# Second early expert with its rows as stationary operand, and full tails in the first Fourier transform

## The chip, the cores and the metric

The kernel runs on one core of one Trainium2 chip. The metric is device time in microseconds (us) of one execution, as a median of several. The engines are named as in the profile: PE (TensorE, with PEld for its weight loads), DVE (VectorE), ACT (ScalarE), POOL (GpSimd) and SP (SyncE, which here only asks for DMA transfers).

## The reference

Attention over 576 positions in 4 batches and 8 heads of 64, each query looking at the last 128 keys; a mixing layer with a Fourier transform over positions and features, a normalisation and an MLP; and a layer of 8 experts in which each token goes to one.

```python
scores = where(mask, scale * q @ k.T + bias, -1e9)          # rel in [0, 128)
x = (softmax(scores) @ v)                                    # (4, 576, 512)

X = np.fft.fft(np.fft.fft(x, axis=1), axis=2)
u = x + np.real(X)
un = (u - mean(u)) / sqrt(var(u) + 1e-6)
x = u + np.maximum(un @ w_ch1, 0.0) @ w_ch2                  # 512 -> 2048 -> 512

e = argmax(logits[b, s]) if s == 0 or local_gate[b, s] < 0.5 else prev_e
h = np.maximum(x[b, s] @ w1[e], 0.0)                         # 512 -> 1024
out[b, s] = p[e] * (h @ w2[e])                               # 1024 -> 512
```

## The kernel before

**Products.** Operands are split into a rounded high part (a copy on ACT, line 171) and a low part (a subtraction on DVE, or POOL where that is asked for, line 172). `mm3` makes three products of one (lines 175 to 177): high by high, high by low, low by high. The Fourier products are not split: they are plain float32 matmuls, each of which appears as two records in the trace.

**Stages.** The first batch's attention and transform stand in a hand-written order in `opening`. The other batches' attention and transforms run beside the first half of the MLP, the second half follows with routing beside it. Then come the experts: an early one (-1, 256 rows), chosen before routing has ended, a second early one (-2, `NEXT` = 128 rows), and then `r` = 0 to 7, of which 0 and 1 reuse the weights of -1 and -2. A loop calls the generator of the running stage, and between its steps lets the generators in `beside` (routing, gathers and transposes of the next rows) and `pre_` (weights of the next expert) make a step. That alone sets the order; each engine runs its instructions in the order in which they were written.

**Experts.** `ffn` takes `xT`, the gathered rows turned and split. For each of eight blocks of 128 hidden features (`f`), a tile of the first weights is the stationary operand and the rows move: 4 x 3 matmuls of as many columns as there are rows, into a PSUM tile `hps`. ACT's relu makes the high part (line 642), DVE the low part (line 645). A step later the block's hidden rows are the stationary operand of the second products, `acc`, 512 columns each. Weights come in four chunks of 256 hidden features (`t1`, `t2`).

`expert_inputs(r)` prepares the rows of expert `r` in steps: ids, then one gather (an indirect DMA on POOL, tile `xg`, line 1292) a step, then one `transpose_split` a step (four transposes into `tps`, line 614, and a split into `xTe`). `last["rows"]` holds the instruction for which the first weight load of `r` = 2 waits on SP's queue.

**The first transform.** Positions are folded about the middle, so that the sum runs over 289 instead of 576 positions: two tiles of 128 and a tail (`kt` = 2) of 33 positions for the cosine part and 32 for the sine part. `fold` makes the folded tile `xf` on DVE (lines 509 to 519; in `opening` some of it on POOL), with one copy of a row on ACT (line 511). The sine part's tail is put on partitions from 64, with the table `tab1` copied there. The features are folded too, into two blocks of 128 and one lone column (`PART`), so that `zprod` (line 588 in `mixing`, line 906 in `opening`) has five products per `kt`: blocks 0 and 1 for cosine and sine, and the lone column for cosine. Each has the folded tile as the stationary operand and 289 columns of the table moving.

Of the kernel before, what the change touches and what calls it, by code (L numbers as in the profile page):

```python
# [111 lines left out]
def constants():  # L112
# [16 lines left out]
    tab1[64:, 1, 2] = tab1[:64, 1, 2]  # L129
# [34 lines left out]
def build(ctx, tc, a, out):  # L164
# [332 lines left out]
    PART = (slice(0, P), ODD, slice(P, P + 1))  # L497

    def fold(xs, kt, eng=nc.vector):
# [4 lines left out]
        o = 64 if kt == 2 else 0  # L504
# [11 lines left out]
        nc.vector.tensor_tensor(out=xo[o:o + m], in0=xa[0:m], in1=xb[0:m], op=ALU.subtract)  # L516
        nc.vector.tensor_tensor(out=xo[o:o + m, 1:HN], in0=xo[o:o + m, 1:HN], in1=xo[o:o + m, DM - 1:HN:-1], op=ALU.subtract)
        eng.tensor_tensor(out=xo[o:o + m, ODD], in0=xo[o:o + m, 1:P + 1], in1=xo[o:o + m, HN - 1:P - 1:-1], op=ALU.add)
        eng.tensor_tensor(out=xo[o:o + m, 1:P], in0=xo[o:o + m, 1:P], in1=xo[o:o + m, HN - 1:P:-1], op=ALU.subtract)
        yield xf  # L520

    def halves(xf, kt):

        n, m = ROWS[kt]
        return slice(0, n), slice(64, 64 + m) if kt == 2 else slice(0, m)
# [48 lines left out]
    def mixing(b):  # L574
# [6 lines left out]
        def zprod(part, kt):  # L581
            xf = zin[kt]
            for cs, db in part:
                w = P if db < 2 else 1
                if kt == 0:
                    pss[cs, db] = ps_g.tile([P, DM], F32, tag="g", name="zps")
                r = halves(xf, kt)[cs]
                nc.tensor.matmul(pss[cs, db][0:w, 0:K1], lhsT=xf[r, cs, PART[db]], rhs=tab1[r, cs, kt], start=kt == 0, stop=kt == 2)  # L588
# [36 lines left out]
    def ffn(xT, n, chunks, ps_h, acc, hidden, sums, tail=0, tags=("acc0", "acc1", "acc2", "g")):  # L625
# [6 lines left out]
        for f in range(nf + 1):  # L632
# [16 lines left out]
            if f > 0:  # L649
# [3 lines left out]
                for t, c in enumerate(range(0, n, P)):  # L653
                    if g == 0:
                        acc.append(sums[t % len(sums)].tile([P, DM], F32, tag=tags[t], name="acc"))
# [6 lines left out]
                yield  # L662

# [10 lines left out]

    rows_of, room, placed = {}, [], []
# [177 lines left out]
    def opening():  # L853
# [47 lines left out]
        def zprod(kt, css=(0, 1)):  # L901
            for (cs, db), ps in bank.items():
                if cs in css:
                    w = P if db < 2 else 1
                    r = halves(got[kt], kt)[cs]
                    nc.tensor.matmul(ps[0:w, 0:K1], lhsT=got[kt][r, cs, PART[db]], rhs=tab1[r, cs, kt], start=kt == 2, stop=kt == 0)

# [315 lines left out]
    per = CB // P  # L1223
# [185 lines left out]
    def expert_inputs(r):  # L1409
# [14 lines left out]
        for t in range(nt):  # L1424
            with nullcontext() if r > 1 else tc.issue_after(last["ffn" if r else "acc"].ins):
# [28 lines left out]
    acc = []  # L1454
# [117 lines left out]
```

## Time and profile before

| what | value |
|---|---|
| median of three runs | 953.61 us (952.82 to 954.89) |
| the profiled execution | 954.66 us, its span 952.8 us, mean granted clock 0.98 |
| PE busy | 902.1 us, 95% |
| DVE busy | 521.9 us, 55% |
| ACT busy | 380.9 us, 40% |
| POOL busy | 246.0 us, 26% |

Matmuls are pipelined: a row's duration overlaps the next row, so the distance between two starts tells what a matmul costs. A row with "x4" joins four like instructions in a row. In brackets stands how long the engine was idle before, and what ended that. A row that joins several shapes shows the shape of the first of them.

### The profile page before, as it was taken

Reading aid. Unit: us, or ns where it says so; the run is one execution under the profiler, and the core shown is the slowest. Engines: PE = TensorE matmul, PEld = TensorE weight load, DVE = VectorE, ACT = ScalarE, POOL = GpSimd, SP = SyncE. Lnnn points to the kernel's source line nnn. Section 1 sums busy time; section 2 is a strip of 40 time slices with the busy share of each in tenths; the row PEclk is TensorE's granted clock in tenths of the full one; section 3 lists DMA queues with packets and bytes.
Section 4 is the critical chain, followed back from the end, with each engine's and each line's share of the span. In section 5 each row is a group of like instructions: output and inputs, shape, how many; then the busy total and the mean of one; then the engine's idle time right before and its main releaser. Section 6 shows DMA issues by size and latency. Waiting matters only on the chain.

```text
span 952.8 us, 16351 instructions
## 1 busy us (share of the span) xinstructions
PE 902.1 (95%) x5992; PEld 749.9 (79%) x5996; DVE 521.9 (55%) x1348; ACT 380.9 (40%) x1001; POOL 246.0 (26%) x369
## 2 busy tenths in 40 slices
PE   7888899999999999999999999999999999999993
PEld 4646577677787898899888888888888898888783
DVE  5788766757656468521333535366763655555410
ACT  4674563663552255421121111114533555455411
POOL 2323641250322046310111223123230312122100
PEclk9998899999999999999999999999999999999997
DMA  9923161451313494253544351446624755455100
GB/s 316 357 84 123 41 203 34 145 175 47 116 42 100 129 339 147 67 155 67 112 111 106 76 102 51 111 111 194 206 95 151 246 189 194 152 199 179 66 20 20
DMA packets 103360, 128.06 MB, mean 134 GB/s; under 512 B 10576, under 2 KB 72400, under 8 KB 103238
## 3 DMA queue, kind: packets, MB, share of 16 engines
q1 hardware_dynamic: 77958, 102.84, 32.8%
q0 software_dynamic: 22720, 19.36, 9.4%
q10 hardware_dynamic: 2592, 4.72, 1.3%
q8 instruction: 49, 0.80, 0.4%
q14 instruction: 41, 0.34, 0.1%
HBM read 98.55 MB, written 30.19 MB: 135 GB/s over the span
## 4 chain that ended last, share of the span: by engine, by line
PE 70%; DVE 12%; issue 7%; DMA 5%; ACT 2%; POOL 2%; SPq 0%; POOLq 0%; DVEq 0%; ACTq 0%
PE hps L175 9%; PE hps L176 9%; PE hps L177 9%; PE acc L175 9%; PE acc L176 8%; PE acc L177 8%; PE o L438 3%; PE zps L588 2%; PE tps L614 2%; PE s L395 2%; DVE t L285 1%; PE acc L659 1%; PE pt L419 1%; DMA r<-ud 1%; PE xps L458 1%
## 5 line engine op out<-in xcount | busy, mean ns | idle before, releaser
L642 ACT ACTIVATE h<-hps 128x256 fp32r<-128x256 f32 (+1 forms) x160 | 60.5, 378 | 287.9 <-PE hps L177 284.6
L645 DVE SCALAR_TENSOR_TENSOR h<-hps,h 128x256 fp32r<-128x256 f32 (+1 forms) x160 | 66.1, 413 | 174.2 <-ACT h L642 173.7
L175 PE MATMUL acc<-t,h 128*128 128x512 f32 x312 | 130.1, 417 | 1.1 <-ACT t L171 1.0
L176 PE MATMUL acc<-t,h 128*128 128x512 f32 x312 | 124.5, 399 | 0.3 <-POOL t L172 0.3
L177 PE MATMUL acc<-t,h 128*128 128x512 f32 x312 | 124.5, 399 | 0.1
L172 DVE TENSOR_TENSOR t<-we,t 128x512 fp32r<-128x512 f32 x128 | 84.1, 689 | 42.1 <-ACT t L171 37.9
L176 PE MATMUL hps<-xTe,t 128*128 128x256 f32 (+7 forms) x320 | 91.8, 287 | 0.3 <-DVE xTe L172 0.3
L175 PE MATMUL hps<-xTe,t 128*128 128x256 f32 (+7 forms) x320 | 91.9, 288 | 0.0
L177 PE MATMUL hps<-xTe,t 128*128 128x256 f32 (+7 forms) x320 | 91.7, 287 | 0.0
L177 PE MATMUL hps<-xT,t 128*128 128x256 f32 x288 | 82.9, 288 | 4.4 <-POOL t L172 4.4
L175 PE MATMUL hps<-xT,t 128*128 128x256 f32 x288 | 84.6, 294 | 1.8 <-ACT t L171 1.5
L171 ACT CAST t<-we 128x512 fp32r<-128x512 f32 x128 | 74.0, 618 | 30.4 <-PE acc L659 17.1
L175 PE MATMUL hps<-xTb,t 128*128 128x256 f32 x288 | 83.1, 288 | 0.0
L176 PE MATMUL hps<-xT,t 128*128 128x256 f32 x288 | 82.7, 287 | 0.0
L177 PE MATMUL hps<-xTb,t 128*128 128x256 f32 x288 | 81.9, 284 | 0.0
L176 PE MATMUL hps<-xTb,t 128*128 128x256 f32 x288 | 81.8, 284 | 0.0
L410 ACT ACTIVATE t<-t,mx 128x128 f32<-128x128 f32 (+1 forms) x160 | 62.6, 394 | 34.9 <-DVE mx L403 30.8
L177 PEld LDWEIGHTS acc<-t,h 128*128 128x128 f32 x312 | 59.1, 190 | 14.6 <-issue 0.7
L175 PEld LDWEIGHTS acc<-t,h 128*128 128x128 f32 x312 | 59.3, 190 | 14.2 <-issue 4.7
L176 PEld LDWEIGHTS acc<-t,h 128*128 128x128 f32 x312 | 59.5, 191 | 7.8 <-POOL t L172 0.6
L175 PEld LDWEIGHTS hps<-xTe,t 128*128 128x128 f32 x320 | 60.6, 190 | 4.1 <-ACT xTe L171 0.4
L176 PEld LDWEIGHTS hps<-xTe,t 128*128 128x128 f32 x320 | 60.6, 190 | 3.1 <-DVE xTe L172 0.5
(293 smaller groups left out, 1999.1 us busy)
## 6 DMA issues: line engine op xcount, KB each, us to landing
we<-in_w SPq DMA_DIRECT2D x64, 512.0 KB
rw<-in_w_ch SPq DMA_DIRECT2D x32, 512.0 KB
qkt<-in_qk SPq DMA_DIRECT2D x15, 642.0 KB
nd<-xT SPq DMA_DIRECT2D x18, 512.0 KB
xTb<-nd POOLq DMA_DIRECT2D x18, 512.0 KB
vt<-in_v SPq DMA_DIRECT2D x16, 384.0 KB
pd<-y ACTq DMA_DIRECT2D x18, 256.0 KB
ub<-ud SPq DMA_DIRECT2D x18, 256.0 KB
```

The lines of the kernel that those rows point to most:

```text
L171: last["hi"] = nc.scalar.copy(hi, src)
L172: return (eng or nc.vector).tensor_tensor(out=lo, in0=src, in1=hi.bitcast(F32), op=ALU.subtract)
L175: nc.tensor.matmul(o, lhsT=wh, rhs=xh, start=start, stop=False, **kw)
L176: nc.tensor.matmul(o, lhsT=wh, rhs=xl, start=False, stop=False, **kw)
L177: return nc.tensor.matmul(o, lhsT=wl, rhs=xh, start=False, stop=stop, **kw)
L395: nc.tensor.matmul(o[h], lhsT=qt[r, x, q0:q0 + m], rhs=qt[r, x, k0:k0 + n0 + n1], start=i > 0, stop=True)
L410: nc.scalar.activation(t[0:m, j], t[0:m, j], AF.Exp, bias=mx[0:m, j:j + 1], scale=-1.0, accum_out=sums[0:m, j:j + 1])
L438: nc.tensor.matmul(o[h * D:(h + 1) * D, x, 0:m], lhsT=v[:, OWN[i] - z, (2 * x + h) * D:(2 * x + h + 1) * D], rhs=w[:, z, 2 * h + x, 0:m], ...
L588: nc.tensor.matmul(pss[cs, db][0:w, 0:K1], lhsT=xf[r, cs, PART[db]], rhs=tab1[r, cs, kt], start=kt == 0, stop=kt == 2)
L614: nc.tensor.transpose(ps[:, k, 0:n], src[0:n, k * P:(k + 1) * P], ident[0:n, 0:n])
L642: last["relu"] = nc.scalar.activation(h[:, 0:n], hps[:, 0:n], AF.Relu)
L645: last["rest"] = nc.vector.scalar_tensor_tensor(out=h[:, lo:lo + c1 - c0], in0=hps[:, c0:c1], scalar=0.0, in1=h[:, c0:c1].bitcast(F32), op ...
```

## The change

Three things are changed.

First, expert -2 runs through a new generator, `ffn_rows`. The rows are the stationary operand and the first weights move, a chunk (256 hidden features) at a time: `hide` makes 12 matmuls and a relu into `hn`, `turned` makes two transposes of the chunk's result and a split of it on ACT and DVE, `add` the second products of the chunk as before. Step `i` does `hide` of chunk `i`, `turned` of `i` - 1, `add` of `i` - 2. The steps that `beside` makes in this stage stand elsewhere: the transposes of expert 0's rows at n = 9 instead of 14, and `last["rows"]` is the fourth `hide`'s relu (n = 6) instead of the split that stands last behind the drained generators.

Second, in `r` = 1 the generator `beside` makes steps at n = 0 to 2 and from 9 on, instead of from 2 on.

Third, the tails of the first transform are made full: `xf` of `kt` = 2 is set to zero on POOL (128 x 1024) before its fold, the sine part lies on partitions from 0, and all products take 128 partitions and 128 columns. The lone column's product writes 128 rows, of which one is read.

```diff
-    PART = (slice(0, P), ODD, slice(P, P + 1))
+    PART = (slice(0, P), ODD, slice(P, 2 * P))
@@ fold
-        o = 64 if kt == 2 else 0
+        if kt == 2:
+            nc.gpsimd.memset(xf, 0.0)
...
-        nc.vector.tensor_tensor(out=xo[o:o + m], in0=xa[0:m], in1=xb[0:m], op=ALU.subtract)
+        nc.vector.tensor_tensor(out=xo[0:m], in0=xa[0:m], in1=xb[0:m], op=ALU.subtract)
...
@@ mixing, zprod
-                nc.tensor.matmul(pss[cs, db][0:w, 0:K1], lhsT=xf[r, cs, PART[db]], rhs=tab1[r, cs, kt], start=kt == 0, stop=kt == 2)
+                nc.tensor.matmul(pss[cs, db][:, 0:K1], lhsT=xf[:, cs, PART[db]], rhs=tab1[:, cs, kt], start=kt == 0, stop=kt == 2)
@@ opening, zprod
-                    nc.tensor.matmul(ps[0:w, 0:K1], lhsT=got[kt][r, cs, PART[db]], rhs=tab1[r, cs, kt], start=kt == 2, stop=kt == 0)
+                    nc.tensor.matmul(ps[:, 0:K1], lhsT=got[kt][:, cs, PART[db]], rhs=tab1[:, cs, kt], start=kt == 2, stop=kt == 0)
@@
+    def ffn_rows(xT, chunks, acc):
+        nf = len(chunks)
+        hn, ht = {}, {}
+
+        def hide(c):
+            hps = ps_h[c % len(ps_h)].tile([P, DM], F32, tag="h", name="hps")
+            t1 = chunks[c][0]
+            for k in range(4):
+                last["ffn"] = mm3(hps[:, 0:CB], xT[:, 0, k], xT[:, 1, k], t1[:, 0, k], t1[:, 1, k], k == 0, k == 3)
+            hn[c] = hidden()[:, 0].bitcast(F32)
+            last["relu"] = nc.scalar.activation(hn[c], hps[:, 0:CB], AF.Relu)
+
+        def turned(c):
+            ps = ps_g.tile([P, per, P], F32, tag="g", name="hT")
+            h = hn.pop(c)
+            for j in range(per):
+                nc.tensor.transpose(ps[:, j], h[:, j * P:(j + 1) * P], ident)
+            ht[c] = hidden().rearrange("p h (j n) -> p h j n", j=per)
+            last["rest"] = split(ht[c][:, 0], ht[c][:, 1], ps)
+
+        def add(c):
+            h, t2 = ht.pop(c), chunks[c][1]
+            for j in range(per):
+                last["acc"] = mm3(acc, h[:, 0, j], h[:, 1, j], t2[:, 0, j], t2[:, 1, j], c == 0 and j == 0, c == nf - 1 and j == per - 1)
+
+        for i in range(nf + 2):
+            for c, part in ((i, hide), (i - 1, turned), (i - 2, add)):
+                if 0 <= c < nf:
+                    part(c)
+                    yield
@@ expert_inputs
-            with nullcontext() if r > 1 else tc.issue_after(last["ffn" if r else "acc"].ins):
+            with nullcontext() if r > 2 else tc.issue_after(last["ffn" if r else "acc"].ins):
@@ the second early expert
-    for n, _ in enumerate(ffn(xTs.pop(-2), NEXT, chunksE[-2], ps_h, acc, hidden, (ps_a2,), tags=("acc2",))):
+    acc = ps_a2.tile([P, DM], F32, tag="acc2", name="acc")
+    for n, _ in enumerate(ffn_rows(xTs.pop(-2), chunksE[-2], acc)):
...
-        if n == 14:
+        if n == 6:
+            last["rows"] = last["relu"]
+        if n == 9:
             beside.step(TM)
     beside.drain()
     pre_.drain()
-    last["rows"] = last["hi"]
@@ experts 0 to 7
-            if n >= 2:
+            if n >= 2 if r != 1 else n < 3 or n > 8:
                 beside.step()
```

How that stands on the engines. On PE at the end of the second early expert, before (`hps`: first products, `acc`: second products, `tps`: transposes of expert 0's rows; the last two rows are expert 0's first products):

```order
L177 MATMUL hps_8101<-xTe_7538,t1_7545 128x128
L175 MATMUL acc_8002<-t2_7546,h_8095 128x512
L176 MATMUL acc_8002<-t2_7546,h_8095 128x512
L177 MATMUL acc_8002<-t2_7546,h_8095 128x512
L614 MATMUL tps_8120<-ident_169,xg_7978 128x128 x4
L614 MATMUL tps_8127<-ident_169,xg_7980 128x96 x4
L175 MATMUL acc_8002<-t2_7546,h_8114 128x512
L176 MATMUL acc_8002<-t2_7546,h_8114 128x512
L177 MATMUL acc_8002<-t2_7546,h_8114 128x512
L175 MATMUL hps_8147<-xTe_7977,t1_7138 128x224
L175 MATMUL hps_8163<-xTe_7977,t1_7138 128x224
```

and after (`hT`: the new transposes of a chunk's result):

```order
L673 MATMUL hT_8053<-ident_169,h_8024 128x128 x2
L174 MATMUL acc_7962<-t2_7546,h_8029 128x512
L175 MATMUL acc_7962<-t2_7546,h_8029 128x512
L176 MATMUL acc_7962<-t2_7546,h_8029 128x512
L174 MATMUL acc_7962<-t2_7546,h_8029 128x512
L175 MATMUL acc_7962<-t2_7546,h_8029 128x512
L176 MATMUL acc_7962<-t2_7546,h_8029 128x512
L673 MATMUL hT_8065<-ident_169,h_8051 128x128 x2
L607 MATMUL tps_8071<-ident_169,xg_7982 128x128 x4
L607 MATMUL tps_8078<-ident_169,xg_7984 128x96 x4
L174 MATMUL acc_7962<-t2_7548,h_8056 128x512
```

The transposes of expert 0's rows stand ahead of the last twelve second products instead of the last three, and the second products come in sixes.

On POOL in the opening, before (the `AFFINE_SELECT`s mask attention weights, lines 518 and 519 belong to the folds):

```order
L424 AFFINE_SELECT w<-w 128x512
L426 AFFINE_SELECT w<-w 128x512
L424 AFFINE_SELECT w<-w 128x512
L426 AFFINE_SELECT w<-w 128x512
L518 TENSOR_TENSOR xf<-xf 32x128
L519 TENSOR_TENSOR xf<-xf 32x127
L518 TENSOR_TENSOR xf<-xf 128x128
```

and after:

```order
L423 AFFINE_SELECT w<-w 128x512
L425 AFFINE_SELECT w<-w 128x512
L423 AFFINE_SELECT w<-w 128x512
L425 AFFINE_SELECT w<-w 128x512
L504 MEMSET xf 128x1024
L518 TENSOR_TENSOR xf<-xf 32x128
L519 TENSOR_TENSOR xf<-xf 32x127
L518 TENSOR_TENSOR xf<-xf 128x128
```

The memset is queued behind the last masks and ahead of the tail's fold on POOL.

On PE in expert 1, before, in the second of its four chunks (`tps`: transposes of expert 2's rows, one of them with what follows and one behind the second products):

```order
L176 MATMUL hps_8475<-xTe_8190,t1_7541 128x256
L177 MATMUL hps_8475<-xTe_8190,t1_7541 128x256
L614 MATMUL tps_8493<-ident_169,xg_8440 128x128 x4
L175 MATMUL acc_8424<-t2_7542,hE_8455 128x512
L176 MATMUL acc_8424<-t2_7542,hE_8455 128x512
L177 MATMUL acc_8424<-t2_7542,hE_8455 128x512
L175 MATMUL acc_8428<-t2_7542,hE_8455 128x512
L176 MATMUL acc_8428<-t2_7542,hE_8455 128x512
L177 MATMUL acc_8428<-t2_7542,hE_8455 128x512
L614 MATMUL tps_8508<-ident_169,xg_8460 128x128 x4
L175 MATMUL hps_8515<-xTe_8190,t1_7543 128x256
```

and after, in the third of the four:

```order
L175 MATMUL hps_8490<-xTe_8150,t1_7547 128x256
L176 MATMUL hps_8490<-xTe_8150,t1_7547 128x256
L607 MATMUL tps_8508<-ident_169,xg_8372 128x128 x4
L174 MATMUL acc_8394<-t2_7548,hE_8474 128x512
L175 MATMUL acc_8394<-t2_7548,hE_8474 128x512
L176 MATMUL acc_8394<-t2_7548,hE_8474 128x512
L174 MATMUL acc_8398<-t2_7548,hE_8474 128x512
L175 MATMUL acc_8398<-t2_7548,hE_8474 128x512
L176 MATMUL acc_8398<-t2_7548,hE_8474 128x512
L607 MATMUL tps_8523<-ident_169,xg_8392 128x128 x4
L174 MATMUL hps_8530<-xTe_8150,t1_7549 128x256
```

The rows read alike; the transposes stand a whole chunk, 24 first and 12 second products, later.

## Rows read from the trace of the kernel before

**Rows 1.** The page: busy time of each engine and its share of the span.

```profile
PE 902.1 (95%) x5992; PEld 749.9 (79%) x5996; DVE 521.9 (55%) x1348; ACT 380.9 (40%) x1001; POOL 246.0 (26%) x369
```

**Rows 2.** PE's timeline, end of second early expert: start, duration, what [idle before].

```profile
724.93 0.48 PE L175 MATMUL hps<-xTe,t 128*128 128x224 f32 x2
725.74 0.37 PE L176 MATMUL hps<-xTe,t 128*128 128x224 f32 x1 [0.33 <-DVE xTe L172]
```

**Rows 3.** The timelines of Pool and PE in expert 1.

```profile
753.11 1.44 POOL L1292 DMA_INDIRECT xg<-x2d,idn  x1 [1.81 <-issue]
...
758.47 0.63 PE L614 MATMUL tps<-ident,xg 128*128 128x128 f32 x4 [1.46 <-DMA xg<-x2d,idn]
```

**Rows 4.** Windows: busy us by engine, granted clock (PEclk), DMA share.

```profile
220.00:240.00 20.00, 20.00 (x103) 12.81 (x104) 14.25 (x37) 8.49 (x34) 1.36 (x4) 1.00 0.11 34
...
312.00:314.00 2.00, 2.00 (x6) 1.25 (x4) 0.20 (x1) 0.00 (x0) 0.00 (x0) 0.50 0.27 82
```

**Rows 5.** PE's timeline around the fourth batch's transform.

```profile
308.82 1.43 PE L588 MATMUL zps<-tab,xf 33*128 33x289 f32 x4 [0.75 <-DVE xf L514]
310.18 0.66 PE L614 MATMUL tps<-ident,u 128*128 128x128 f32 x4
310.74 5.22 PE L588 MATMUL zps<-tab,xf 128*128 128x289 f32 x12
315.89 0.38 PE L175 MATMUL hps<-xT,t 128*128 128x256 f32 x1
```

**Rows 6.** PE's timeline, one block in the second early expert.

```profile
711.04 0.23 PE L175 MATMUL hps<-xTe,t 128*128 128x128 f32 x1
...
712.61 0.40 PE L176 MATMUL acc<-t,h 128*128 128x512 f32 x1
...
713.08 0.22 PE L175 MATMUL hps<-xTe,t 128*128 128x128 f32 x1
```

**Rows 7.** PE's timeline in expert 1, products of 256 columns.

```profile
748.34 0.28 PE L175 MATMUL hps<-xTe,t 128*128 128x256 f32 x1
...
751.21 0.40 PE L175 MATMUL acc<-t,hE 128*128 128x512 f32 x1
```

**Rows 8.** PE's timeline, a pair of transposes in the first early expert.

```profile
689.28 0.38 PE L1107 MATMUL tp<-ident,oh 128*8 128x128 f32 x2
...
689.96 0.28 PE L175 MATMUL hps<-xTe,t 128*128 128x256 f32 x1
```

**Rows 9.** ScalarE's timeline, both early experts.

```profile
705.08 0.39 ACT L642 ACTIVATE h<-hps 128x256 fp32r<-128x256 f32 x1 [1.43 <-PE hps L177]
...
709.31 0.61 ACT L171 CAST t<-we 128x512 fp32r<-128x512 f32 x1
```

**Rows 10.** PE's timeline, second batch's transform.

```profile
160.82 0.65 PE L588 MATMUL zps<-tab,xf 128*1 128x289 f32 x2
161.40 0.39 PE L176 MATMUL hps<-xT,t 128*128 128x256 f32 x1
...
161.97 1.14 PE L588 MATMUL zps<-tab,xf 128*128 128x289 f32 x4
...
163.18 0.40 PE L177 MATMUL acc<-t,h 128*128 128x512 f32 x1
```

**Rows 11.** Pool's groups, then Pool's and VectorE's timelines, fourth transform.

```profile
L301 POOL MEMSET zn<- 128x384 f32 x1 | 0.4, 419 | 0.3 <-POOLq L1552 0.3
...
304.62 0.28 POOL L714 TENSOR_SCALAR v<-v 128x2 f32<-128x2 f32 x1
...
305.54 0.67 DVE L509 TENSOR_TENSOR xf<-x 32x512 f32<-32x512 f32 x1
```

**Rows 12.** Pool's, VectorE's and PE's timelines in the opening.

```profile
43.58 0.64 POOL L426 TENSOR_SCALAR_AFFINE_SELECT w<-w 128x512 f32<-128x512 f32 x1
...
43.97 0.78 DVE L509 TENSOR_TENSOR xf<-x 32x512 f32<-32x512 f32 x1
...
46.85 0.44 PE L458 MATMUL xps<-ident,ot 128*128 128x128 f32 x2 [0.62 <-DVE ot L446]
```

More of the change, by code (lines that the diff above doesn't have):

```diff
@@ L128, in constants @@
     tab2[P - 1, 1, KE:] *= 0.5
-    tab1[64:, 1, 2] = tab1[:64, 1, 2]
     c["tab1"] = tab1.astype(np.float32)
@@ L515, in fold @@
         yield
-        nc.vector.tensor_tensor(out=xo[o:o + m], in0=xa[0:m], in1=xb[0:m], op=ALU.subtract)
-        nc.vector.tensor_tensor(out=xo[o:o + m, 1:HN], in0=xo[o:o + m, 1:HN], in1=xo[o:o + m, DM - 1:HN:-1], op=ALU.subtract)
-        eng.tensor_tensor(out=xo[o:o + m, ODD], in0=xo[o:o + m, 1:P + 1], in1=xo[o:o + m, HN - 1:P - 1:-1], op=ALU.add)
-        eng.tensor_tensor(out=xo[o:o + m, 1:P], in0=xo[o:o + m, 1:P], in1=xo[o:o + m, HN - 1:P:-1], op=ALU.subtract)
+        nc.vector.tensor_tensor(out=xo[0:m], in0=xa[0:m], in1=xb[0:m], op=ALU.subtract)
+        nc.vector.tensor_tensor(out=xo[0:m, 1:HN], in0=xo[0:m, 1:HN], in1=xo[0:m, DM - 1:HN:-1], op=ALU.subtract)
+        eng.tensor_tensor(out=xo[0:m, ODD], in0=xo[0:m, 1:P + 1], in1=xo[0:m, HN - 1:P - 1:-1], op=ALU.add)
+        eng.tensor_tensor(out=xo[0:m, 1:P], in0=xo[0:m, 1:P], in1=xo[0:m, HN - 1:P:-1], op=ALU.subtract)
         yield xf
-    def halves(xf, kt):
-        n, m = ROWS[kt]
-        return slice(0, n), slice(64, 64 + m) if kt == 2 else slice(0, m)
     def combine(xs, Z, kb):
@@ L623, in shift_of, with ffn @@
         return -(-m // 32) * 32
-    def ffn(xT, n, chunks, ps_h, acc, hidden, sums, tail=0, tags=("acc0", "acc1", "acc2", "g")):
+    def ffn(xT, n, chunks, ps_h, acc, hidden, sums, tail=0):
         per = CB // P
@@ L654, in ffn @@
                     if g == 0:
-                        acc.append(sums[t % len(sums)].tile([P, DM], F32, tag=tags[t], name="acc"))
+                        acc.append(sums[t % len(sums)].tile([P, DM], F32, tag=("acc0", "acc1", "acc2", "g")[t], name="acc"))
                     m = min(P, n - c)
@@ L673, in behind @@
         return st
+    per = CB // P
     rows_of, room, placed = {}, [], []
@@ L1220, in rank @@
         eb.append(nc.values_load(eid[0:1, 2, r:r + 1], engines=SP, min_val=0, max_val=(E - 1) * CAP + EARLY))
-    per = CB // P
     ring = [wpA] * nA + [wpB] * nB
@@ L1463, in build @@
     pre_.drain()
-    last["rows"] = last["hi"]
     with tc.issue_after(last["hi"].ins):
-        emit(acc[0], ids[-2][:, 0])
+        emit(acc, ids[-2][:, 0])
     chunksE[0], chunksE[1] = chunksE[-1], chunksE[-2]
```

5 lines of the change are left out of this document (removed).

## Prediction

> **What bounds the kernel now.** The busy line of the page comes first: TensorE works 95% of the span [rows 1]. So what counts is the number of matmuls, the distance between their starts, and the few places where PE waits. I therefore read PE's timeline at each place that the change touches, taking the distance between starts as the price of a matmul (the durations overlap), and then the engines that feed it there. At the end of the second early expert PE waits for VectorE [rows 2], in the middle of expert 1 for a gather [rows 3]; around the third batch's transform it does not wait at all [rows 4]; in the fourth's it first waits for VectorE and then runs slowly [rows 5].
>
> **The second early expert.** Before, eight blocks of 12 products of 128 columns and 3 of 512 follow each other; one block is 713.08 - 711.04 = 2.04 us [rows 6], the stage 8 x 2.04 = 16.32 us without the eight transposes for expert 0's rows, which stay. After, there are 48 products of 256 columns, at (751.21 - 748.34) / 24 = 0.12 us each [rows 7]: 5.76. The 24 second products stay, at (713.08 - 712.61) / 2 = 0.235 [rows 6]: 5.64. Eight transposes are added, in four pairs; a pair between second products lies in a stretch of 689.96 - 689.28 = 0.68 us that also holds two products of 512, so it costs 0.68 - 0.47 = 0.21 [rows 8]: 0.84. Together 12.24, a gain of 4.1.
>
> At the stage's end two products of expert 0 take 725.74 - 724.93 = 0.81 us where two of their size take some 0.22 (twice 0.11, by 0.12 for 256 columns); the third is held by xTe's low part, split on VectorE [rows 2]. After, those rows' transposes stand ahead of the last 12 second products (12 x 0.235 = 2.8 us of cover), so 0.5 of it goes. **Sum -4.6 us**; bounds: -4.1 if that wait stays, -5.1 if the changes between kinds of product in the old block (12 to 3 and back, eight times) cost more than I count.
>
> What could eat it is the new chain: relu, transposes, split, second products. The relu of 256 columns takes 0.39 on ScalarE, a cast of 512 columns, the nearest row to the split, 0.61 [rows 9]. Beside the relu PE has the next chunk's 12 products (1.44 us), beside the split 6 second products or 12 first ones (1.4). I charge nothing; without that cover it would be about a microsecond a chunk. ScalarE's next cast may stand ahead of a relu once: +0.6 at most, inside the bounds.
>
> The weights of expert 2 are released by the fourth relu, not by the last split: halfway through the stage. No wait of PE stands on them, so it is worth nothing; the gathers queued on Pool's DMA queue do not wait for SP's load.
>
> **Expert 1.** The gathers for expert 2 begin at 753.11 on Pool, and PE waits 1.46 us for the first of them at 758.47: 5.36 us from issue to transposes [rows 3]. After, they are asked at the first steps and the transposes stand one chunk later: 24 first products of 0.12 and 12 second ones of 0.235, 5.7 us of PE's work, far over 1.46. What is late next is the last transpose of the four, now a chunk nearer to expert 2's first product, with its split (0.6 on ScalarE, then VectorE) behind it. I take **-1.4**, bounds -0.5 (the splits late at expert 2's start, where 0.5 was seen at expert 0's [rows 2], and as much again) and -1.46.
>
> **Full tails in the transforms.** A product becomes no shorter in columns moved, 289 in each case. Four full records between others take 163.18 - 161.97 - 0.235 = 0.975, or 0.244 each; two records with one stationary column take 161.40 - 160.82 = 0.58, so 0.09 more than 0.49 on leaving the form, and the same on entering [rows 10]. Four records on 33 and 32 rows take 310.18 - 308.82 = 1.36 where four full ones take 0.975: 0.385 more, in four steps of some 0.1 [rows 5]. A transform holds two such sets of four and three pairs of one column: at most 2 x 0.385 + 3 x 0.18 = 1.3, and 0.2 less where two odd forms stand side by side. **-1.1** for the second batch's transform and **-1.1** for the third's, around which PE is busy 20.00 of 20 us [rows 4]. Each also gets a memset of 128x1024 on Pool. The only wide memset, 128x384, takes 0.419 us [rows 11]; in proportion that makes 1.1, as the estimate, and less if part of it is fixed. In these two batches nothing on Pool or VectorE stands near, so it is hidden; if not, each costs up to 1.1.
>
> In the fourth batch's, VectorE's fold of the tail starts at 305.54, and Pool is busy until 304.90 [rows 11]; a memset of 1.1 behind it ends at 306.0, so the fold is 0.45 late, and PE's wait of 0.75 for it grows by that [rows 5]. Against it stand the two sets of four behind the wait, 0.77. **-0.35**, bounds -0.8 and +0.4.
>
> In the opening the memset is queued behind Pool's mask at 43.58 (0.64 us), ends near 45.3, and the fold of the tail on VectorE, at 43.97 before, waits that long: 1.35 [rows 12]. All of VectorE's queue behind it is late by as much, among it the copy that PE awaits at 46.85. PE then saves its own 1.1. **+0.3**, bounds 0 and +1.35: the saving may turn into waiting for the next fold.
>
> **The clock.** From 310.74 on, twelve records take 315.89 - 310.74 = 5.15 us [rows 5]; at 0.244 and with 0.35 for the four on part of the rows it would be 3.3. In 312:314 the granted clock is 0.50, the 1.2 GHz level [rows 4], right behind the wait of 0.75 and products on a quarter of the rows [rows 5]. So 1.9 us were lost to the low clock. Filled, those products keep the whole array at work, and the wait alone is short beside the work around it: I take **-1.9**, bounds 0 and -1.9. This is a choice that no row settles. By the Trainium skill, "TensorE: Matmul & The Clock Gate", section "What's actually happening", the clock follows how busy TensorE has recently been; by that rule products on few rows count as busy like any, filling them would buy nothing, the wait alone would have caused the fall, and the sum would be 1.9 higher. The trace of before cannot separate the two.
>
> **Sum.** -4.6 - 1.4 - 1.1 - 1.1 - 0.35 + 0.3 - 1.9 = -10.15. The profiled run took 954.66 us, so the forecast is **944.5**; that run lies 1.05 above the median of the three, from which it would be 943.5.
>
> **The rivals.**
> 1. *The clock falls all the same*, at 311 or, with everything moved by some microseconds, elsewhere. For it: the wait in the fourth transform, now 1.2 us. Against it: the filled rows. 944.5 + 1.9 = 946.4.
> 2. *The transforms' gain does not reach the end*: in the opening the full 1.35 is paid, and the 2.2 of the two middle transforms go into waits for VectorE's folds, which are unchanged. For it: PE's wait for VectorE in the fourth [rows 5]; against it: 20.00 of 20 us busy around the third [rows 4]. 944.5 + 1.05 + 2.2 = 947.8.
> 3. *Half of the second early expert's gain goes into the new chain*, if ScalarE's casts stand ahead of the relus: 944.5 + 2.3 = 946.8.
> 4. *Slower*: the chain becomes serial, each chunk's second products waiting for relu (0.39), transposes (0.21 and their way), split (0.61, then VectorE's share) and what is queued ahead on both, about 3 us with the crossings, four times. 12 us give 956.5. It decides when each chunk waits over 10.15 / 4 = 2.5 us. Against it: first products of the next chunk always stand between.
> 5. *Nothing of it shows*: the shorter stages only move the waits to the experts' weights, whose loads are not sped up: 953.6.
>
> **How the numbers follow.** Forecast 0.48, clock 0.27, transforms 0.12, half the chain 0.08, slower 0.03, nothing 0.02. The forecast's own bounds are 942.5 (the better ends of the expert and of the fourth transform, and the distance to the median in part) to 946. The range goes from 941.8 to 948.3, which takes in rivals 1 to 3 with half a microsecond. A difference of 0.2%, 1.9 us, is about what a measurement of this kernel can tell from none. Faster by over that 0.94, within it 0.03, slower 0.03.
>
> **What would show it.** Right: in the second early expert 48 first products 0.12 apart, second ones in groups of six with no wait over 0.2 us on ScalarE or VectorE, and a stage some 4.1 us shorter; at expert 0's start no wait on xTe; in expert 1 no wait on xg; all records of the transforms with one form, 0.244 apart; a granted clock of 1.00 from 308 to 316. Wrong: waits "<-ACT h" or "<-DVE" at the new transposes or at their second products; a clock of 0.50 behind the fourth transform's fold or in a new place; PE idle over 1 us behind VectorE in the opening or in the middle transforms; expert 2's first products held by xTe.

## The result, and the profile after

| | before | after |
|---|---|---|
| median, measured side by side | 954.1 us (4 runs) | 943.53 us (4 runs, 938.02 to 944.96) |
| ratio | | 0.988, 95% interval 0.9838 to 0.9921 |
| the profiled execution, its span | 954.66, 952.8 | 942.90, 941.2 |
| with the runs beside the experiments | 954.6, median of 34, 948.71 to 958.79 | 942.2, median of 10, 938.02 to 944.96 |

The forecast was 944.5, the range 941.8 to 948.3. The kernel became 10.6 us faster, 1.1%, and the largest terms came out as worked out. With the runs beside the experiments the difference is 12.4. One term, the clock, was right for this pair of executions by its amount; its reason is not borne out by the runs.

Where the time went is read by the start of like instructions in the two profiles (the start after, less the start before). A step of the last column is what the stretch up to there gave or cost.

| place | before | after | difference | step |
|---|---|---|---|---|
| opening, last turned tile before the transform | 44.11 | 44.29 | +0.18 | |
| opening, behind its transform | 59.67 | 59.94 | +0.27 | +0.1 |
| first half, ahead of the second batch's transform | 113.3 | 111.7 | -1.62 | -1.9 |
| first product of that transform | 158.28 | 156.45 | -1.83 | -0.2 |
| behind that transform | 172.4 | 169.9 | -2.44 | -0.6 |
| behind the third batch's | 245.1 | 241.2 | -3.98 | -1.5 |
| ahead of the fourth batch's | 303.15 | 299.30 | -3.85 | +0.1 |
| behind it | 317.42 | 311.06 | -6.36 | -2.5 |
| output of the first early expert | 707.2 | 700.5 | -6.63 | -0.3 |
| output of the second early expert | 725.0 | 714.2 | -10.79 | -4.2 |
| output of expert 0 | 747.8 | 736.2 | -11.64 | -0.85 |
| output of expert 1 | 773.5 | 760.2 | -13.32 | -1.7 |
| last output of expert 5 | 894.4 | 881.0 | -13.42 | -0.1 |
| output of expert 6 | 915.7 | 903.9 | -11.84 | +1.6 |

The steps of -1.9 and -0.2 ahead of the second batch's transform are no work of the change: before, the granted clock is 0.50 from 106.4 to 113.2, after from 105.1 to 108.5.

The line of the page that answers to [rows 1]:

```profile
PE 891.7 (95%) x5956; PEld 748.4 (80%) x5956; DVE 519.7 (55%) x1344; ACT 380.8 (40%) x1001; POOL 249.0 (26%) x373
```

PE is busy 10.4 us less and the span is 11.6 shorter, so the gain is nearly all busy time of PE, products made slow by the low clock counted in; the share of 95% stays.

PE in the second early expert and at the start of expert 0, answering to [rows 2, 6, 8] (start, duration, what, [idle before]):

```profile
701.02 0.28 PE L174 MATMUL hps<-t,xTe 128*128 128x256 f32 x1
...
703.89 0.38 PE L673 MATMUL hT<-ident,h 128*128 128x128 f32 x2
704.03 0.36 PE L174 MATMUL hps<-t,xTe 128*128 128x256 f32 x1
...
705.54 0.38 PE L673 MATMUL hT<-ident,h 128*128 128x128 f32 x2
...
710.20 0.38 PE L673 MATMUL hT<-ident,h 128*128 128x128 f32 x2
710.41 0.93 PE L607 MATMUL tps<-ident,xg 128*128 128x128 f32 x8
711.13 0.47 PE L174 MATMUL acc<-t,h 128*128 128x512 f32 x1
...
713.98 0.26 PE L174 MATMUL hps<-xTe,t 128*128 128x224 f32 x1
714.08 0.28 PE L175 MATMUL hps<-xTe,t 128*128 128x224 f32 x1
```

The stage runs from 701.02 to 713.98, 12.96 us with the eight transposes for expert 0's rows (711.13 - 710.41 = 0.72). A pair of new transposes between first products takes 704.03 - 703.89 = 0.14 and another 0.08 at the product behind it, about the 0.21 of the forecast. No row of PE in the stage has a wait. Expert 0's first two products stand 0.10 apart, and nothing holds the third.

ScalarE beside it, answering to [rows 9]:

```profile
704.09 0.38 ACT L667 ACTIVATE h<-hps 128x256 f32<-128x256 f32 x1 [0.55 <-PE hps L176]
704.37 0.61 ACT L170 CAST t<-we 128x512 fp32r<-128x512 f32 x1
704.88 0.38 ACT L170 CAST h<-hT 128x256 fp32r<-128x256 f32 x1
```

The split of a chunk (`h<-hT`, 0.38) is shorter than the cast that was taken for it. Ahead of the first chunk's split (704.88) stand a relu and a cast of the next weights, and PE does not wait for that either: the first products of the third chunk, from 704.03 to 705.54, are its cover.

Expert 1, answering to [rows 3], Pool first:

```profile
740.61 1.00 POOL L1314 DMA_INDIRECT xg<-x2d,idn  x1 [0.96 <-PE hps L176]
...
750.85 0.60 PE L607 MATMUL tps<-ident,xg 128*128 128x128 f32 x4
```

The gather is issued at 740.61 and the transposes stand at 750.85, 10.2 us later, with no wait.

The second batch's transform and the third's, answering to [rows 10]: of each the first products and those that follow the transform, first before, then after:

```profile
158.28 1.82 PE L588 MATMUL zps<-tab,xf 128*128 128x289 f32 x6
...
172.36 0.49 PE L534 MATMUL pc<-tab,z 128*128 128x128 f32 x2
...
224.54 1.82 PE L588 MATMUL zps<-tab,xf 128*128 128x289 f32 x6
...
245.15 0.38 PE L534 MATMUL pc<-tab,z 128*128 128x128 f32 x2
```

```profile
156.45 1.73 PE L581 MATMUL zps<-tab,xf 128*128 128x289 f32 x6
...
169.92 0.49 PE L529 MATMUL pc<-tab,z 128*128 128x128 f32 x2
...
222.01 1.73 PE L581 MATMUL zps<-tab,xf 128*128 128x289 f32 x6
...
241.17 0.38 PE L529 MATMUL pc<-tab,z 128*128 128x128 f32 x2
```

The second batch's takes 13.47 us instead of 14.08, the third's 19.16 instead of 20.61, with the other work that stands among their products.

The fourth transform, answering to [rows 5, 11], PE, then Pool's memset and VectorE's fold of the tail, and the windows behind it, answering to [rows 4] (busy us and instructions of PE, PEld, DVE, ACT, POOL, then the granted clock):

```profile
303.93 0.75 PE L581 MATMUL zps<-tab,xf 128*128 128x289 f32 x2 [0.78 <-DVE xf L512]
304.87 1.24 PE L581 MATMUL zps<-tab,xf 128*128 128x289 f32 x4 [0.19 <-DVE xf L514]
305.94 0.60 PE L607 MATMUL tps<-ident,u 128*128 128x128 f32 x4
306.60 3.19 PE L581 MATMUL zps<-tab,xf 128*128 128x289 f32 x12
...
301.28 0.94 POOL L504 MEMSET xf<- 128x1024 f32 x1
...
302.25 0.68 DVE L509 TENSOR_TENSOR xf<-x 32x512 f32<-32x512 f32 x1 [0.21 <-POOL xf L504]
...
304.54 0.27 DVE L514 TENSOR_TENSOR xf<-xf 33x128 f32<-33x128 f32 x1
```

```profile
306.00:308.00 2.00, 1.95 (x11) 1.44 (x10) 1.13 (x3) 1.19 (x3) 0.00 (x0) 1.00 0.04 8
308.00:310.00 2.00, 2.00 (x12) 1.62 (x11) 0.06 (x1) 0.58 (x2) 0.00 (x0) 1.00 0.33 102
```

The memset (0.94 us) makes VectorE's first row wait 0.21. PE waits 0.78 and 0.19, where it waited 0.75 and, ahead of the products at 307.43, 0.15 before. All records have one form; the clock is 1.00 throughout, and the last twelve records last 3.19 us instead of 5.22. The row of the same fold that PE awaited before, for the account below:

```profile
308.48 0.28 DVE L514 TENSOR_TENSOR xf<-xf 33x128 f32<-33x128 f32 x1
```

The opening, answering to [rows 12], Pool, VectorE and PE:

```profile
44.33 0.95 POOL L504 MEMSET xf<- 128x1024 f32 x1
...
45.32 0.68 DVE L509 TENSOR_TENSOR xf<-x 32x512 f32<-32x512 f32 x1 [1.08 <-POOL xf L504]
...
48.10 0.44 PE L457 MATMUL xps<-ident,ot 128*128 128x128 f32 x2 [1.68 <-DVE ot L445]
```

The fold is at 45.32 instead of 43.97, and PE's wait for the copy `ot` is 1.68 instead of 0.62.

### The profile page after: what moved, and what is told of

Same layout as the page of the kernel before. It is cut to its first block, busy times and chain, and to the rows that moved or that the text cites. A ratio compares the mean times of both kernels' runs of the same rounds, so it can differ in the third digit from the quotient of the medians.

```text
span 941.2 us, 16266 instructions
## 1 busy us (share of the span) xinstructions
PE 891.7 (95%) x5956; PEld 748.4 (80%) x5956; DVE 519.7 (55%) x1344; ACT 380.8 (40%) x1001; POOL 249.0 (26%) x373
## 4 chain that ended last, share of the span: by engine, by line
PE 68%; DVE 13%; issue 8%; DMA 4%; POOL 4%; ACT 2%; SPq 0%; POOLq 0%; DVEq 0%; ACTq 0%
PE hps L174 9%; PE hps L176 9%; PE hps L175 9%; PE acc L174 8%; PE acc L175 8%; PE acc L176 8%; PE s L394 3%; PE o L437 2%; PE zps L581 2%; DVE t L284 2%; PE tps L607 2%; PE acc L652 1%; PE pt L418 1%; POOL t L171 1%; DVE t L400 1%
## 5 line engine op out<-in xcount | busy, mean ns | idle before, releaser
L635 ACT ACTIVATE h<-hps 128x256 fp32r<-128x256 f32 x152 | 58.3, 383 | 273.6 <-PE hps L176 270.2
L638 DVE SCALAR_TENSOR_TENSOR h<-hps,h 128x256 fp32r<-128x256 f32 x152 | 63.7, 419 | 159.5 <-ACT h L635 159.1
L174 PE MATMUL hps<-xTe,t 128*128 128x256 f32 (+6 forms) x288 | 83.9, 291 | 0.0
L175 PE MATMUL hps<-xTe,t 128*128 128x256 f32 (+6 forms) x288 | 83.4, 290 | 0.0
L176 PE MATMUL hps<-xTe,t 128*128 128x256 f32 (+6 forms) x288 | 83.2, 289 | 0.0
L176 PEld LDWEIGHTS acc<-t,h 128*128 128x128 f32 x312 | 58.9, 189 | 14.9 <-DVE h L638 1.3
L638 DVE SCALAR_TENSOR_TENSOR hE<-hps,hE 128x256 fp32r<-128x256 f32 (+3 forms) x96 | 29.8, 338 | 61.4 <-ACT hE L635 61.1
L174 PEld LDWEIGHTS hps<-xT,t 128*128 128x128 f32 x288 | 55.3, 192 | 8.6 <-ACT t L170 2.8
```

The source lines that it names most:

```text
L174: nc.tensor.matmul(o, lhsT=wh, rhs=xh, start=start, stop=False, **kw)
L175: nc.tensor.matmul(o, lhsT=wh, rhs=xl, start=False, stop=False, **kw)
L176: return nc.tensor.matmul(o, lhsT=wl, rhs=xh, start=False, stop=stop, **kw)
L635: last["relu"] = nc.scalar.activation(h[:, 0:n], hps[:, 0:n], AF.Relu)
L638: last["rest"] = nc.vector.scalar_tensor_tensor(out=h[:, lo:lo + c1 - c0], in0=hps[:, c0:c1], scalar=0.0, in1=h[:, c0:c1].bitcast(F32), op ...
```

## The experiments

**The parts alone.** One kernel has the changed expert part and the old transforms, one the full tails and the old expert part.

```diff
# expert part alone: the tails as before
-    PART = (slice(0, P), ODD, slice(P, 2 * P))
+    PART = (slice(0, P), ODD, slice(P, P + 1))
...
# full tails alone: the second early expert and expert 1 as before
-    for n, _ in enumerate(ffn_rows(xTs.pop(-2), chunksE[-2], acc)):
+    for n, _ in enumerate(ffn(xTs.pop(-2), NEXT, chunksE[-2], ps_h, acc, hidden, (ps_a2,), tags=("acc2",))):
...
-            if n >= 2 if r != 1 else n < 3 or n > 8:
+            if n >= 2:
```

> Both expert parts of the change alone; the transforms are as before. Theory: up to the end of the first early expert the trace is that of the kernel before (difference under 0.3 us at like clock), then the second early expert is 4.2 us shorter, expert 0 begins without the wait on xTe (0.8) and expert 1 without the wait on xg (1.7 with what stands behind it), so 6.5 us in all: about 947.5. In the fourth transform the granted clock may fall to 0.50 again. Rival (part of the gain needs the transforms to be shorter): under 5 us.

> The full tails alone; the expert part is as before. Theory: opening +0.3, second batch's transform -0.6, third's -1.4, fourth's -0.6 at like clock, and another -1.9 if the clock does not fall there: 2.3 without the clock, 4.2 with it, so 949.5 to 952. Rival (the clock is not tied to the filled tails): the granted clock is 0.50 behind the fourth transform's wait in this kernel too, and the gain at like clock is all there is.

The expert part alone: 947.84 us, ratio 0.9936 (0.9908 to 0.9965). From the first early expert's output to expert 1's the starts move by -4.17, -0.85 and -1.68 against the kernel before, 6.7 us together, and then stay to the end. That is the whole chain of the forecast's expert terms in one trace, within a hundredth what the changed kernel shows. The full tails alone: 947.36 us, ratio 0.9934 (0.9912 to 0.9957). By their trace the second batch's transform gives 0.6, the third's 1.5, the fourth's 2.9, of which 1.75 is the clock: 5.0 together. The median lies 2.1 below the 949.5 to 952 that was expected; these terms do not make that up, and the mean granted clock of those runs is higher over the whole execution (0.985 against 0.983 before). The two ratios multiply to 0.987; the parts add up.

**The clock behind the fourth transform.** The kernel after and the kernel before were run again, unaltered, for further profiles.

> The changed kernel once more, unaltered, so that two profiled executions of it can be laid side by side. Theory (the clock's falls differ from execution to execution, while the work is the same): the starts of like instructions differ by under 0.3 us wherever both run at the same granted clock; the stretches at 1.2 GHz lie elsewhere or are longer or shorter by several us, and the time of each execution falls with its mean granted clock, by about 9 us for 0.01. Rival (each kernel has its own fixed falls): the same stretches as in the first profile of it, and times within 2 us. Median 940 to 945.

> The kernel before once more, for a third profiled execution with the tails unfilled. If the fall behind the fourth transform's wait belongs to the kernel, the granted clock is 0.50 there as in the first profile and in that of the expert parts alone; if it is a matter of where that place falls in time, it may be 1.00, and the transform is then 1.7 to 1.9 us shorter.

The changed kernel again: 941.43 us, ratio 0.9865 (0.9831 to 0.99). At expert 6's start both of its executions have the same wait at nearly the same time. First the execution of the first profile, then the repeated one (a PE row each, and the window behind it):

```profile
882.05 0.50 PE L174 MATMUL acc<-t,hE 128*128 128x512 f32 x1 [1.05 <-ACT hE L635]
...
884.00:886.00 2.00, 2.00 (x8) 1.65 (x7) 0.00 (x0) 0.00 (x0) 0.00 (x0) 0.50 0.01 0
```

```profile
882.02 0.50 PE L174 MATMUL acc<-t,hE 128*128 128x512 f32 x1 [1.06 <-ACT hE L635]
...
884.00:886.00 2.00, 2.00 (x16) 1.87 (x15) 0.00 (x0) 0.21 (x1) 0.00 (x0) 1.00 0.01 0
```

The same kernel waits 1.05 us at 882.05 and runs at 0.50 behind it, and waits 1.06 at 882.02 and runs at 1.00. The fall costs 1.6 us: that is the +1.6 in the last line of the table of differences. So this fall belongs to the execution, not to the kernel. Times go with it: over the 34 runs of the kernel before, a mean clock lower by 0.01 goes with 6.1 us more (a straight line through them), and the ten of the changed kernel give 6.9 (9 was expected).

The kernel before again, 951.77 us in its one run, has the wait of 0.75 and the partly filled products in its fourth transform, and no fall:

```profile
305.90 1.43 PE L588 MATMUL zps<-tab,xf 33*128 33x289 f32 x4 [0.75 <-DVE xf L514]
...
308.00:310.00 2.00, 2.00 (x9) 1.29 (x9) 0.69 (x1) 0.56 (x2) 0.00 (x0) 1.00 0.00 0
```

From the first product of the fourth transform to its end it is 1.75 us shorter than in the first profile of the same kernel. The expert part alone, with the same transform, has the fall:

```profile
310.32 1.43 PE L588 MATMUL zps<-tab,xf 33*128 33x289 f32 x4 [0.75 <-DVE xf L514]
...
314.00:316.00 2.00, 2.00 (x5) 0.95 (x5) 0.00 (x0) 0.00 (x0) 0.00 (x0) 0.50 0.49 153
```

Four more kernels look for what makes the difference: products on 33 and 32 rows with 128 columns, with a small memset and with the whole one, products on one column with all rows (twice), and a wait three memsets long.

```diff
# rows partial (the second kernel keeps the whole memset)
-            nc.gpsimd.memset(xf, 0.0)
+            nc.gpsimd.memset(xf[:, :, P:2 * P], 0.0)
...
-  ... lhsT=xf[:, cs, PART[db]], rhs=tab1[:, cs, kt] ...
+  ... lhsT=xf[0:ROWS[kt][cs], cs, PART[db]], rhs=tab1[0:ROWS[kt][cs], cs, kt] ...
# one column
-    PART = (slice(0, P), ODD, slice(P, 2 * P))
+    PART = (slice(0, P), ODD, slice(P, P + 1))
...
-  ... pss[cs, db][:, 0:K1] ...
+  ... pss[cs, db][0:P if db < 2 else 1, 0:K1] ...
# long wait (times is 3 for the fourth batch, else 1)
-            nc.gpsimd.memset(xf, 0.0)
+            for _ in range(times):
+                nc.gpsimd.memset(xf, 0.0)
```

> The changed kernel with the tail's products on 33 and 32 of the 128 rows again (both halves on partitions from 0), while all stationary operands keep 128 columns; the memset covers the lone block alone. Theory of the prediction (products on a quarter of the rows helped the clock to fall): the granted clock is 0.50 for some 3.4 us behind the fourth transform's wait, and like clock apart each transform loses the part of its gain that lay in the rows, 0.3 to 0.8. Rival (the wait alone decides, or where it falls in time): the clock stays at 1.00 there, as in the four executions with full tails, and only 0.3 to 0.8 per transform is lost. Median 943 to 947.

> As the kernel with the tail's products on 33 and 32 rows and full columns, but with the memset of the whole tile, so that PE's wait in the fourth transform is the changed kernel's 0.8 to 1.0 instead of 0.7. If partial rows help the clock to fall once the wait is as long as in the kernel before (0.9 with the short one ahead of it), the granted clock is 0.50 there; if rows do not matter, it stays 1.00 and the transform is only 0.3 to 0.7 longer than the changed kernel's.

> The changed kernel with the lone block's products on one stationary column again (one row of output written); all rows stay filled. First theory (products on one column help the clock to fall, as in the kernel before and with the expert parts alone): the granted clock is 0.50 for some 3.4 us behind the fourth transform's wait, and the next stage starts 1.7 to 2.3 us later than in the changed kernel at like clock ahead of it. Second theory (neither rows nor columns; the wait and where it falls in time): the clock stays 1.00 there; only the changes of form come back, 0.2 to 0.6 per transform.

> The same kernel as the one before it in this call, for a second profiled execution, since the falls of the clock differ between executions. By the first theory the fall is there in both, by the second in neither; in one of the two only would mean that the columns do not settle it.

> The changed kernel with the fourth transform's memset made three times (0.95 us each), so that the fold of the tail and PE behind it are 1.9 us later; all products stay full. Rival on the clock (idle time of PE brings the fall): PE waits 2.7 us there instead of 0.8 and the granted clock falls to 0.50 behind it, for 1.9 us of wait and another 1.7 of slow products: the next product after the transform 3.6 us later than in the changed kernel. Theory of the prediction (full products keep the clock up): the wait grows by 1.9, the clock stays 1.00, and that is all. Median 943 to 947.

Partial rows: 944.84 us, ratio 0.9914 (0.9887 to 0.9941), clock 1.00 behind a wait of 0.49 + 0.19. Against the first profile of the changed kernel its transforms are 0.5 (opening), 0.4, 1.0 and 0.4 us longer at like clock: the filled rows are worth that much. Partial rows with the whole memset: 948.06 in one run (its profile has a long stretch at 0.50 in the opening, from 48.7 to 58.9), and in the fourth transform, PE and then the window:

```profile
310.71 0.75 PE L581 MATMUL zps<-tab,xf 33*128 33x289 f32 x2 [0.79 <-DVE xf L512]
311.65 1.43 PE L581 MATMUL zps<-tab,xf 33*128 33x289 f32 x4 [0.19 <-DVE xf L514]
...
312.00:314.00 2.00, 2.00 (x10) 1.09 (x9) 1.24 (x3) 0.88 (x3) 0.00 (x0) 1.00 0.29 104
```

One column: 941.17 and 943.38, one run each, clock 1.00 in both behind waits of 0.26 + 0.29 and 0.19 + 0.29; the second batch's and the third's transform are 0.4 and 0.5 longer than in the changed kernel, the price of the one column. The long wait: 943.97 us, ratio 0.9897 (0.9873 to 0.9922), with its fall:

```profile
307.92 0.76 PE L582 MATMUL zps<-tab,xf 128*128 128x289 f32 x2 [2.80 <-DVE xf L513]
...
310.00:312.00 2.00, 2.00 (x8) 1.57 (x7) 0.00 (x0) 0.70 (x2) 0.00 (x0) 0.50 0.03 8
```

There all products are full, and PE's wait of 2.80 us is followed by 0.50; the next stage starts 3.2 us later than in the first profile of the changed kernel, 2.0 for the wait and 1.2 for the clock (3.6 later than in the second, 2.1 and 1.5). Laid side by side:

| kernel, executions profiled | tail products | waits of PE in the fold, us | clock behind |
|---|---|---|---|
| before; expert part alone | partial rows, one column | 0.75, and 0.15 or 0.11 ahead of it | 0.50 in both |
| before, again | the same | 0.75 | 1.00 |
| changed (2); full tails alone; early memset; serial chain; free output tile | full | 0.69 to 0.79, and 0.18 or 0.19 | 1.00 in all six |
| partial rows (2 kernels) | partial rows, 128 columns | 0.49 and 0.79, and 0.19 | 1.00 in both |
| one column (2) | all rows, one column | 0.19 and 0.26, and 0.29 | 1.00 in both |
| long wait | full | 2.80 and 0.19 | 0.50 |

A fall can follow idle time of PE without any partial product. Partial products with a wait do not always bring one (the kernel before, again). Neither partial rows alone nor one column alone brought it, in two executions each; but only one of these four, partial rows with the whole memset, had a wait as long as in the kernel before, so the single column is not tested at that wait. With both, two of three executions fell, with full tails none of six at an ordinary wait; whether filling lowers the chance of a fall, or three executions are too few to say, stays open. The mean granted clock of whole executions leans to the former: 0.983 over the 34 runs of the kernel before and 0.981 over the 9 of the expert part alone, 0.985 over the 10 of the changed kernel and the 12 of the full tails alone; at 6 us for 0.01 the difference is 1.2 us or more. A mean does not say where the clock fell, though: the free output tile has full tails and 0.984 (5 runs), and partial rows have 0.983 (8 runs) with no fall at this place in the profile.

The same traces hold a second place to compare. Some 45 us behind the fourth transform PE waits 1.98 to 2.00 us ahead of transposes (`tps<-ident,u`) that are the same in every kernel, at 362.44 in the first profile of the kernel before and at 356.05 in that of the changed one. The clock behind it is 0.50 in six of the fourteen executions (before, expert part alone, early memset, serial chain, one column twice) and 1.00 in the other eight, the kernel before again and the changed kernel twice among them. Full and unfilled tails stand on both sides: like products behind a like wait fall in one execution and not in the next. By the Trainium skill, "TensorE: Matmul & The Clock Gate", section "What's actually happening", the clock follows how busy TensorE has recently been, and what watches it does not start anew with the kernel, so that the point at which the clock changes differs from run to run. The long wait agrees with the first, the two executions of the changed kernel with the second.

**The opening's memset.** It is queued on Pool ahead of the last two pairs of masks.

```diff
-    def fold(xs, kt, eng=nc.vector):
+    def fold(xs, kt, eng=nc.vector, xf=None):
...
+            if n == 18:
+                xf2 = slab([P, 2, DM], F32, "xf", "m", MB)
+                nc.gpsimd.memset(xf2, 0.0)
             if n == 23:
-                folds.append((2, fold(xs, 2, nc.gpsimd)))
+                folds.append((2, fold(xs, 2, nc.gpsimd, xf2)))
```

> The changed kernel with the opening's memset queued on Pool ahead of the last two pairs of masks instead of behind them. Theory: the fold of the tail on VectorE starts 1.35 us earlier than in the changed kernel, PE's wait of 1.68 for the copy ot falls to 0.6, and the first transform ends some 1.1 us earlier: about 1 us less in the end. Rival (the opening's end is set by something else, VectorE's later folds or the converted weights): the wait of 1.68 falls but the transform's end moves by under 0.4. Second rival: the memset delays the masks and PE's products with w by up to 0.95.

```profile
46.79 0.44 PE L457 MATMUL xps<-ident,ot 128*128 128x128 f32 x2 [0.62 <-DVE ot L445]
...
57.68 0.49 PE L530 MATMUL pc<-tab,z 128*128 128x128 f32 x2 [0.55 <-ACT z L937]
```

941.67 us, ratio 0.9867 (0.9827 to 0.9906): no difference in time from the changed kernel that the runs can tell. In the trace PE's wait for `ot` is 0.62 again, so the copy and all products of the transform are 1.07 us earlier than in the changed kernel. But PE now waits 0.55 for ScalarE's copy of `z` behind the transform, and what comes next starts only 0.34 earlier. The rival holds: two thirds of the memset's price in the opening were hidden, by ScalarE's work, in the changed kernel already.

**The chain made serial.** Each chunk's three parts are written one behind the other.

```diff
-        for i in range(nf + 2):
-            for c, part in ((i, hide), (i - 1, turned), (i - 2, add)):
+        for i in range(nf):
+            for c, part in ((i, hide), (i, turned), (i, add)):
```

> The changed kernel with the second early expert's chain made serial: each chunk's transposes and second products stand right behind its first ones, ahead of the next chunk's. Theory (what hides relu, transposes and split in the changed kernel is the other chunks' products): PE waits for the relu before each chunk's transposes (0.4 and the crossing) and for the split before the second products (0.4 on ScalarE, 0.4 on VectorE and the crossings), some 1.6 to 2.0 us a chunk with PE idle: 6.5 to 8 us longer in the stage, so the gain of the new form is lost there and the stage is slower than before by 2 to 4. Rival (the chain is short): under 1 us a chunk. Median 948 to 951.

PE in that stage:

```profile
703.89 0.44 PE L673 MATMUL hT<-ident,h 128*128 128x128 f32 x2
...
704.64 0.28 PE L176 MATMUL hps<-t,xTe 128*128 128x256 f32 x1
704.79 0.50 PE L174 MATMUL acc<-t,h 128*128 128x512 f32 x1
...
705.36 0.28 PE L174 MATMUL hps<-t,xTe 128*128 128x256 f32 x1
...
715.14 0.37 PE L174 MATMUL hps<-xTe,t 128*128 128x224 f32 x1 [0.51 <-ACT xTe L170]
```

943.34 us, ratio 0.9904 (0.9871 to 0.9937). The second early expert is 2.5 us longer than in the changed kernel (2.2 behind expert 0's start), not 6.5 to 8, and still 1.6 shorter than in the kernel before. The chain did not become serial: between a chunk's transposes (703.89) and its second products (704.79) stand first products of the next chunk (704.64), and again among the second ones (705.36). So it is not true, as the part ahead of the prediction has it, that the order of writing alone sets the order on an engine: in this stage products that were ready stand ahead of products that waited, against the written order. What moves them, the traces do not show. A chain that is serial on the engine was therefore not measured, and the fourth rival stands untested; that the cover is needed is argued from the trace and not shown. What the written order is worth here is the 2.5 us: 0.51 is the one wait in PE's rows (715.14), and the rest lies in the distances between starts, where kinds of product change.

**An output tile that is free.** Beside the early memset, the tail rows' output of an expert takes one of the four hidden tiles, which are unused by then, instead of one of the two that the other outputs use.

```diff
-        y = act.tile([P, DM], F32, tag="y", name="yo")
+        y = act.tile([P, DM], F32, tag="h", name="yo", bufs=HB) if both else act.tile([P, DM], F32, tag="y", name="yo")
```

> The changed kernel with two waits taken away: the opening's memset queued ahead of the last pairs of masks, as before, and the tail rows' output tile of an expert (yo, where both halves are added) taken from the four free hidden buffers instead of from the two that the other output tiles use. Theory: ScalarE's wait of 1.42 for an output transfer goes, with it PE's waits of 1.05 and 0.41 at expert 6's start: 1.4 us less at like clock, and no fall of the clock behind that place (1.6 in the execution that had one); with 0.3 from the opening 1.7 to 3.3 us less than the changed kernel, median 938 to 941. Rival (ScalarE's copy, made earlier, now holds up the relu of the first product or the casts): the waits of PE move by a block and the gain is under 0.5.

ScalarE and PE at expert 6's start:

```profile
876.43 0.58 ACT L1327 COPY yo<-acc 16x512 f32<-16x512 f32 x1
...
878.08 0.36 ACT L636 ACTIVATE hE<-hps 128x232 fp32r<-128x232 f32 x1
...
878.65 0.40 PE L174 MATMUL acc<-t,hE 128*128 128x512 f32 x1
...
879.68 0.50 PE L176 MATMUL acc<-t,hE 128*128 128x512 f32 x1 [0.40 <-DVE hE L639]
```

939.81 us, ratio 0.9865 (0.9843 to 0.9886). ScalarE's copy of the 16 tail rows stands at 876.43 with no wait ahead of the relu at 878.08, and of PE's two waits the one of 1.05 is gone, the one of 0.41 stays. Expert 6's output comes 2.9 us earlier against the place before it, 1.3 for the wait and 1.6 for the fall of the clock that the first profile of the changed kernel had there. The times do not separate it from the changed kernel (ratio 0.9865 there too, measured beside other runs of the kernel before); the trace does, by 1.3 us.

## Why the prediction was right, point by point

- **The second early expert, -4.6.** Measured -4.2 up to the stage's output and -0.85 from there to expert 0's, of which 0.6 is the wait at its start (0.81 against 0.22 before [rows 2], nothing after). The working gave 12.24 us for the new stage without expert 0's transposes; it is 12.96 - 0.72 = 12.24. The old one was 16.56 by its ends, not 16.32. The term came out 0.4 too small, within its bounds. No cost of the new chain showed: PE has no wait there, with the cover that was named beside it.
- **Expert 1, -1.4.** Measured -1.7: the wait of 1.46 is gone [rows 3], and 0.2 more, 0.2 beyond the bound. (In the second execution of the kernel before that wait is 1.73.) Expert 2's first products were not held by the later splits.
- **The middle transforms, -1.1 each.** Measured -0.6 and -1.45, 2.06 together where 2.2 was forecast; each is off by some 0.4, and the third's lies above the 1.3 that was taken as the most. The memsets, 0.95 us where 1.1 was the estimate, were hidden.
- **The fourth transform, -0.35.** Measured -0.8 without the clock (the kernel before, again, against the changed kernel), and -1.1 against the second profile of the changed kernel. The step that was off is the wait: it was to grow by 0.45, and VectorE's fold did start 0.56 late (305.54 - 3.85 = 301.69 against 302.25). But the rows of the fold then stood closer together than before, and its last one (304.54) was 0.1 earlier than before by the same shift (308.48 - 3.85). So the row that PE waited for was not late, and the wait did not grow by what was forecast.
- **The opening, +0.3.** Measured +0.1: 1.07 of wait, paid back by PE's own 1.1. The upper bound, 1.35, was far off.
- **The clock, -1.9.** The fall at 311 was not there after, and the pair of profiles shows 1.75 for it. The reason given, filled products, is not shown: a third execution with unfilled tails had no fall, and partial rows or one column alone had none. That products on few rows count as busy like any, the reading of the rival, is not shown either. What the forecast should have carried is a chance: two falls in three executions of 1.75 make 1.2 at most. The fall at expert 6 took 1.6 back in the profiled execution, a shorter stretch at 0.50 around 106 to 113 gave 2; such changes are as large as this term, and single executions of one kernel differ by 7 us.
- **The sum, -10.15.** The terms that do not hang on the clock are -4.2, -0.85, -1.7, -0.6, -1.45, -0.8 and +0.1, together -9.5, where the forecast had -8.25 for them. The mechanisms of the larger ones were right, and their sizes 1.3 too small together. That the forecast met the median within 1.0 us is partly luck: the clock's -1.9, whose reason is not shown, filled that gap.

## What to carry to other kernels

Where few rows meet many weights, let the rows be stationary and the weights move. Here a product of 128 columns took (2.04 - 3 x 0.235) / 12 = 0.11 us [rows 6] and one of 256 columns 0.12 [rows 7], so half as many products of twice the columns nearly halve the time, and what is added (a turn of the result and its split) costs some 0.84 us in a stage of 13, with another chunk's products beside the chain. Products of one form in a row were cheaper here than smaller ones of another: filling a tail up costs a memset and saves some 0.1 us at each change of form. Before a gain or a loss is put down to the clock, take a second profile of the unchanged kernel: a fall that is in one may be missing in the next.

## What the runs showed that was not expected

- The same wait of PE, 1.05 us at 882, was followed by 0.50 in one execution and by 1.00 in another of the same kernel; single times of one kernel span 7 us (the changed one) and 10 us (the one before).
- VectorE's rows of the tail's fold stand 0.20 apart where the sine part lies on partitions from 0 (304.13, 304.34, 304.54 after), and 0.32 where it lies on partitions from 64 (307.85, 308.17, 308.48 before), with durations of 0.27 and 0.28. So the rows overlap in the first case, and in the second each starts only when the one ahead of it has ended. It is so in the six executions read for it (two of the kernel before, two of the changed one, each part alone); why was not tried. It paid for the memset in the fourth transform.
